# Attention with cached K and V, two problems on one core: first product in token halves, weights on a second DMA queue, half of x transposed by DMA

## The chip, the core and the metric

The kernel runs on one core of one Trainium2 chip. The metric is device time in microseconds (us), from launch to the last store. The engines: TensorE (in the profile PE for matmuls and PEld for weight loads, which overlap the matmuls), VectorE (DVE), ScalarE (ACT), GpSimd (POOL) and SyncE (SP). SP and ACT issue DMA transfers; SPq and ACTq are their queues in the profile, and PEq is TensorE's instruction sequencer. The granted clock is the share of TensorE's full clock that the profile records. A line number such as L306 is a line of the kernel; the changed kernel's lines stand four lower in the steady part (L306 becomes L302).

## The reference, cut to what matters

Two independent problems, A and B, each: 512 tokens (16 batches of 32) by 1024, 32 query heads, 4 K/V heads, 512 cached positions, head width 128, bf16.

```python
q = (x @ wq).reshape(B, Sq, Hq, Dh).transpose(0, 2, 1, 3)
scores = einsum("bhqd,bhkd->bhqk", q, repeat(k_cache)) * Dh ** -0.5
o = einsum("bhqk,bhkd->bhqd", softmax(scores), repeat(v_cache))
out = o.transpose(0, 2, 1, 3).reshape(B, Sq, Hq * Dh) @ wo
```

## The kernel before

The heads 0 to 7 of problem A are computed first ("the start"). After that a loop over 128 attention slots begins; each slot is scores, exponentials and values for one batch and one K/V head, and between them TensorE takes about seven matmuls per slot from one long stream: the query heads 8 to 31 of A, those of B, then the output products. Each query head has eight matmuls, one per chunk of 128 rows of wq. Weights arrive in blocks of four heads, 1 MB each.

The start loads x and the first weights on the sync queue. TensorE warms up on a tile of zeros, transposes all 32 blocks of x and multiplies as the chunks come in:

```python
load_x(0, slice(0, TT // 2)); load_x(0, slice(TT // 2, TT))
load_w0(slice(0, 1), slice(0, NF * DH // 2))          # NF = 6 heads early
...                                                   # the other chunks, x and w0 in turn
load_k(0, slice(0, 1))                                # K by DMA transpose
load_wq(0, 2)                                         # heads 8 to 11
load_k(0, slice(1, GRP)); load_v(0); load_k(1); load_v(1)

warm_up(19)
transpose_x(0, (2, 4))                                # 8 transposes on TensorE, copies on DVE and ACT
for dc in range(DC - 2):
    for h in range(NF):
        if dc % 2 and h == NF // 2:
            transpose_x(dc // 2 + 1)
        first_head(first_q[h], h, dc)
...                                                   # last two chunks, then heads 6 and 7 alone
```

The later loads follow a plan by slot. The stream of projections looks its weights up by name when it is built:

```python
def load_wq(pr, c4, ...):
    t = blk_tile([P, DC, 4 * DH], "wq_sb")
    ...                                               # one DMA of 1 MB
    wq_tiles[pr, c4] = t                              # replaces an older tile of that name

for c4 in range(3, 16):                               # block 3 holds heads 12 to 15
    need = (c4 - 2) * 4 * DC / 7.0
    at(max(0, int(need) - 10), load_wq, c4 // 8, c4 % 8)   # c4 = 3 comes at slot 0
```

## Time and profile before

| | before |
|---|---|
| median of 4 runs | 346.69 us (346.27 to 347.31) |
| profiled execution | span 344.8 us |
| TensorE busy | 336.7 us, 98% |
| head 8 begins (first matmul with wq_sb) | 20.44 us |
| TensorE stops for the block of heads 12 to 15 | 1.58 us, until 31.28 us |

From the page of the kernel before: the first line of the busy table, and the chain of work that ended last.

```profile
PE 336.7 (98%) x2098; PEld 214.2 (62%) x2137; DVE 267.3 (78%) x338; ACT 186.9 (54%) x210; POOL 46.7 (14%) x206
...
PE 89%; SPq 5%; DMA 3%; issue 1%; ACT 0%; ACTq 0%
PE f_ps L325 31%; PE q_ps L306 25%; PE ob L430 17%; PE s_ps L362 16%; SPq L280 4%; DMA wq_sb<-in_A_wq_dram 2%; DMA x_sb<-in_A_x_dram 1%; SPq L471 1%; SPq L468 0%; SPq L288 0%; SPq L250 0%; ACT o_sb L334 0%; SPq L697 0%; ACTq L334 0%
```

TensorE is the limit, but the 11% of the chain that are not TensorE are worth a look: queue issues (SPq, mostly the K transposes of L280) and two DMA landings. Nearly all of it lies in the start. The table of stretches of the kernel before, TensorE only (stretch, its length, busy time and instructions, granted clock, DMA share, GB/s), shows where TensorE is not full:

```profile
0.00:29.70 29.70, 28.26 (x170) 1.00 0.96 240
29.70:31.30 1.60, 0.02 (x1) 1.00 1.09 351
31.30:335.00 303.70, 301.81 (x1869) 1.00 0.87 210
```

After 31.3 us nothing is left to gain by a better start: TensorE is busy to the end. So the time is the moment at which it can go on with head 12, plus what follows (344.8 - 31.3 = 313.5 us). The timeline of the start of the kernel before (start, length, engine, line, operation; in brackets the idle time ahead and what ended it):

```profile
0.86 0.96 SPq L468 DMA_DIRECT2D x_sb<-in_A_x_dram  x2
1.08 2.21 PE L500 MATMUL warm_ps<-warm 128*128 128x128 bf16 x19 [1.08 <-DVE shift L237]
3.40 0.61 PE L514 MATMUL xT_ps<-ident,x_sb 128*128 128x128 bf16 x4
4.95 2.32 PE L526 MATMUL q_ps<-xT,w_sb 128*128 128x512 bf16 x9
...
20.44 1.24 PE L306 MATMUL q_ps<-xT,wq_sb 128*128 128x512 bf16 x5
24.48 3.80 SPq L250 DMA_DIRECT2D wq_sb<-in_A_wq_dram  x3
29.09 0.60 PE L362 MATMUL s_ps<-qT,kT 128*128 128x256 bf16 x4
31.28 1.69 PE L306 MATMUL q_ps<-xT,wq_sb 128*128 128x512 bf16 x7 [1.58 <-DMA wq_sb<-in_A_wq_dram]
```

x lands by 3.40 us, right as the 19 warm-up matmuls end. Head 8 begins at 20.44. The block for heads 12 to 15 is the first of the three issued from 24.48 on, and TensorE waits for it until 31.28.

### The profile page before, as it was taken

To read this page: it belongs to the slowest core of one execution; us is meant where nothing else is said; L and a number is where in the kernel's file an instruction comes from. 1 tells how busy PE (TensorE), PEld (TensorE's weight loads), DVE (VectorE), ACT (ScalarE), POOL (GpSimd) and SP (SyncE) were. 2 spreads that over 40 slices of the span, in tenths; PEclk is the share of its full clock that TensorE was granted. 3 is DMA by queue.
4 is the path that set the end of the run, shared out by engine and by line. 5 is a ranking of instruction groups with operands and counts; after the bars stand their busy time and mean duration, and the time that the engine had idled before them with its cause. 6 is when DMAs were issued, how large, how long until landed. Compare 5 with 4: busy or idle time off the path is not lost.

```text
span 344.8 us, 5491 instructions
## 1 busy us (share of the span) xinstructions
PE 336.7 (98%) x2098; PEld 214.2 (62%) x2137; DVE 267.3 (78%) x338; ACT 186.9 (54%) x210; POOL 46.7 (14%) x206
## 2 busy tenths in 40 slices
PE   8998999999999999999999999999999999999996
PEld 6554666666666666666666666666666666666555
DVE  1236888888988898888888898889888888888540
ACT  2346667667666666666654545554455555554010
POOL 0001110011111111111002212221222100111100
PEclk9999999999999999999999999999999999999999
DMA  6999989899997999999999956999649996440001
GB/s 193 307 174 347 231 241 274 172 290 261 300 273 162 227 243 225 215 214 307 268 282 254 238 137 175 345 248 228 117 107 290 334 187 170 106 109 0 17 18 33
DMA packets 126509, 71.70 MB, mean 208 GB/s; under 512 B 73744, under 2 KB 126224, under 8 KB 126480
## 3 DMA queue, kind: packets, MB, share of 16 engines
q1 hardware_dynamic: 125952, 70.20, 84.1%
q0 software_dynamic: 384, 1.05, 0.8%
q8 instruction: 17, 0.28, 0.4%
q14 instruction: 12, 0.10, 0.1%
q10 hardware_dynamic: 144, 0.07, 0.1%
HBM read 51.38 MB, written 2.10 MB: 155 GB/s over the span
## 4 chain that ended last, share of the span: by engine, by line
PE 89%; SPq 5%; DMA 3%; issue 1%; ACT 0%; ACTq 0%
PE f_ps L325 31%; PE q_ps L306 25%; PE ob L430 17%; PE s_ps L362 16%; SPq L280 4%; DMA wq_sb<-in_A_wq_dram 2%; DMA x_sb<-in_A_x_dram 1%; SPq L471 1%; SPq L468 0%; SPq L288 0%; SPq L250 0%; ACT o_sb L334 0%; SPq L697 0%; ACTq L334 0%
## 5 line engine op out<-in xcount | busy, mean ns | idle before, releaser
L370 ACT ACTIVATE p_sb<-s_ps,shift 128x1024 bf16<-128x1024 f32 x128 | 142.5, 1114 | 103.4 <-PE s_ps L362 85.5
L381 DVE TRANSPOSE_TENSOR_REDUCE parts<-p_sb 128x32 f32<-128x1024 bf16 x128 | 158.9, 1242 | 20.5 <-ACT p_sb L370 18.8
L325 PE MATMUL f_ps<-wo_sb,oT 128*128 128x512 bf16 (+1 forms) x525 | 127.5, 366 | 0.5
L306 PE MATMUL q_ps<-xT,wq_sb 128*128 128x512 bf16 x430 | 113.7, 379 | 2.2 <-DMA wq_sb<-in_A_wq_dram 1.6
L430 PE MATMUL ob<-p_sb,v_sb 128*128 128x256 bf16 x512 | 76.8, 273 | 0.8
L362 PE MATMUL s_ps<-qT,kT 128*128 128x256 bf16 x512 | 76.8, 273 | 0.0
L325 PEld LDWEIGHTS <-oT 128*128 128x128 bf16 x544 | 53.2, 98 | 36.0
L362 PEld LDWEIGHTS <-kT 128*128 128x128 bf16 x512 | 56.8, 113 | 28.6 <-DMA kT<-in_B_k_cache_dram 0.5
L306 PEld LDWEIGHTS <-wq_sb 128*128 128x128 bf16 x448 | 43.7, 98 | 33.4 <-DMA wq_sb<-in_A_wq_dram 1.8
L430 PEld LDWEIGHTS <-v_sb 128*128 128x128 bf16 x512 | 50.1, 98 | 20.0
L452 DVE TENSOR_TENSOR oT<-r,ob 128x512 bf16<-128x512 f32 x64 | 44.0, 687 | 23.4 <-PE ob L430 22.9
L416 DVE STREAM_TRANSPOSE r<-rall 128x512 f32<-128x512 f32 x64 | 44.2, 691 | 1.1
L314 ACT CAST qT<-q_ps 128x512 bf16<-128x512 f32 x56 | 32.6, 582 | 13.8 <-PE q_ps L306 13.8
L399 POOL COPY half<-cs 64x32 f32<-64x32 f32 x32 | 6.5, 204 | 230.6 <-DVE cs L389 230.6
L334 ACT CAST o_sb<-f_ps 128x512 bf16<-128x512 f32 (+1 forms) x17 | 9.5, 558 | 24.4 <-PE f_ps L325 16.7
L526 PE MATMUL q_ps<-xT,w_sb 128*128 128x512 bf16 x62 | 14.4, 383 | 0.2
L389 DVE TENSOR_REDUCE cs<-parts 128x32 f32<-128x128 f32 x32 | 12.1, 377 | 1.1
L411 DVE RECIPROCAL rall<-sums 128x32 f32<-128x32 f32 x32 | 10.2, 318 | 1.6 <-POOL sums L408 1.6
L520 DVE COPY xT<-xT_ps 128x512 bf16<-128x512 bf16 x4 | 1.7, 424 | 11.5 <-PE xT_ps L514 11.5
L526 PEld LDWEIGHTS <-w_sb 128*128 128x128 bf16 x64 | 6.2, 99 | 6.9 <-issue 0.5
L336 POOL DMA_DIRECT2D out_dram<-o_sb x8 | 4.6, 574 | 33.4 <-ACT o_sb L334 33.3
L400 POOL TENSOR_TENSOR half<-half,cs 64x32 f32<-64x32 f32 x32 | 7.8, 242 | 2.6
(26 smaller groups left out, 51.5 us busy)
## 6 DMA issues: line engine op xcount, KB each, us to landing
v_sb<-in_A_v_cache_dram SPq DMA_DIRECT2D x16, 512.0 KB, 4.4
wq_sb<-in_B_wq_dram SPq DMA_DIRECT2D x8, 1024.0 KB, 6.3
wo_sb<-in_A_wo_dram SPq DMA_DIRECT2D x8, 1024.0 KB, 7.5
v_sb<-in_B_v_cache_dram SPq DMA_DIRECT2D x16, 512.0 KB, 4.4
wo_sb<-in_B_wo_dram SPq DMA_DIRECT2D x8, 1024.0 KB, 8.2
wq_sb<-in_A_wq_dram SPq DMA_DIRECT2D x6, 1024.0 KB, 7.5
w_sb<-in_A_wq_dram SPq DMA_DIRECT2D x7, 192.0 KB, 4.9
kT<-in_A_k_cache_dram SPq DMA_TRANSPOSE x64, 4.5
```

The source lines that it names most:

```text
L280: nc.sync.dma_start_transpose(out=kT[:, q, :], in_=ks[q])
L306: nc.tensor.matmul(ps[:], lhsT=w[:, dc, (h % 4) * DH:(h % 4 + 1) * DH], rhs=xT[pr][:, dc, :], start=(dc == 0), stop=(dc == DC - 1),)
L314: nc.scalar.copy(out=qT[pr, g][:, :, hl, :], in_=ps[:].rearrange("p (b s) -> p b s", s=SQ),)
L325: nc.tensor.matmul(ps[:, 0:width], lhsT=oT[pr, tt][:, h, :], rhs=wo_tiles[pr, nh, h // REP][:, h % REP, off:off + width], start=(h == 0), ...
L362: nc.tensor.matmul(s_ps[:, c, :], lhsT=kT[:, i % GRP, c, :], rhs=qT[pr, g][:, b, :, :].rearrange("p h s -> p (h s)"), start=True, stop=True,)
L370: nc.scalar.activation(out=p_sb[:], in_=s_ps[:], func=ACTF.Exp, bias=shift[:], scale=SCALE)
L381: nc.vector.tensor_reduce(out=parts[k][:, q, :, :].rearrange("p c h -> p (c h)"), in_=st[i]["p"][:].rearrange("p c (h s) -> p (c h) s", s=SQ),
L389: nc.vector.tensor_reduce(out=cs[:], in_=parts.pop(k)[:].rearrange("p q c h -> p q h c"), axis=AX.X, op=ALU.add,)
L416: nc.vector.transpose(out=r[:].rearrange("p n s -> p (n s)"), in_=rall[:, k, o * 2 * REP:(o + 1) * 2 * REP] .unsqueeze(2).to_broadcast([P, ...
L430: nc.tensor.matmul(ob[j][:, q, :], lhsT=v_sb[:, i % GRP, c, :], rhs=st[i]["p"][:, c, :], start=(c == 0), stop=(c == KC - 1),)
L452: nc.vector.tensor_tensor(out=out, in0=rcp.pop(j)[:].rearrange("p (q h) s -> p q h s", h=REP), in1=ob.pop(j)[:].rearrange("p q (h s) -> p ...
L526: nc.tensor.matmul(q_ps, lhsT=w0[dc // HC][:, dc % HC, h * DH:(h + 1) * DH], rhs=xT[0][:, dc, :], start=(dc == 0), stop=(dc == DC - 1),)
```

## The change

Its intent is a shorter start: begin the product when half of the tokens of the first x chunk are there, take the first weights from ScalarE's queue so that they are issued beside x, transpose the last four chunks of x by DMA and not on TensorE, and let heads 6 and 7 join at the middle chunk. The block of heads 12 to 15 is also issued early. The core of the diff, cut:

```diff
-            warm = work.tile([P, P], BF16, name="warm", tag="p_sb", bufs=7)
-            nc.vector.memset(warm[:], 0.0)
+            warm = nc.const_aps.tensor(1.0, [P, P], BF16)
...
-            load_x(0, slice(0, TT // 2))
-            load_x(0, slice(TT // 2, TT))
-            load_w0(slice(0, 1), slice(0, NF * DH // 2))
...
+            load_w0(nc.scalar, 0, 1, 0, NF)
+            load_x(0, 0, TT // 2)
+            load_w0(nc.scalar, 1, 2, 0, NF)
+            load_x(0, TT // 2, TT)
+            load_x(2, 0, TT)
...
+            load_x_transposed(HC)
+            load_w0(nc.sync, HC + 2, DC, 0, REP)
+            load_x_transposed(HC + 2)
+            nc.scalar.preload_act_table_set("natural_log_exp_and_others")
             load_wq(0, 2)
+            load_k(0)
+            load_wq(0, 3)
+            load_k(1)
             load_v(0)
...
+            warm_up(23)
+            transpose_x(0, 0, TT // 2)
+            warm_up(3)
+            first_heads(range(0, NF // 2), (0,), 0, TT // 2)
+            transpose_x(0, TT // 2, TT)
+            first_heads(range(NF // 2, NF), (0,), 0, TT // 2)
+            first_heads(range(NF), (0,), TT // 2, TT)
...
+            first_heads(range(NF, REP), range(HC))
+            first_heads(range(REP), range(HC, DC - 2))
...
-                at(GRP * (j - 1) + 2, load_v, j)
+                at(GRP * (j - 1) + 2, load_v, j, 2 if j < 5 else 1)
             for c4 in range(3, 16):
                 need = (c4 - 2) * 4 * DC / 7.0
```

The last two lines are not changed: `load_wq(0, 3)` is new, and the plan's range still begins at 3.

## The prediction

> **What bounds the kernel now.** TensorE: the busy table gives it 336.7 of 344.8 us (98%), and the table by stretches 301.8 of the 303.7 us from 31.3 to 335 us, at granted clock 1.00. Only the start can be shortened. There the timeline shows first transposes 3.40, first product 4.95, head 8 (next weights) 20.2, first scores 21.5 us, and then one wait that matters: TensorE stops from 29.7 to 31.28 for the weight block (wq_sb) of heads 12 to 15, which the sync queue issued at 24.48. The chain of waits says the same: before 31.3 us it runs through sync queue issues (mostly kT transposes, 1.26 to 2.5 us each) and that 6.75 us load. The time is that landing plus a fixed 313 us.
>
> **What the change does.**
> 1. TensorE work at the start shrinks: 16 of 32 transposes go (eight cost about 0.45 us in the stream), -0.9 us; the product starts on the first token half, its weights on ScalarE's queue, about -0.5 us; small waits (0.4 and 0.2 us) may go. Estimate: head 8 at 18.3 to 19 us, unless the DMA-transposed chunks are late (needed near 11.8 and 15, estimated landing 11.5 to 13 and 14 to 15.5). TensorE would be ready for head 12 near 28 us.
> 2. The block for heads 12 to 15 is issued early, but the plan still loads it at slot 0, into a new tile that replaces the first. The instruction order shows that TensorE waits for the second copy and nothing reads the first. So 1 MB is loaded for nothing, ahead of k, v and the copy that counts: 3.1 us at the 340 GB/s that plain loads reached.
> 3. Half of x (0.5 MB) goes through DMA transposes: packets of 256 B took 18 ns against 27 ns for 512 B, so about 0.8 us more DMA time, and two more issues on the sync queue (estimate 2 us each, from 6.8 us for B's 1 MB x). Two early kT transposes each came with a stall of all DMA engines of about 1.2 us; there may be more. The Trainium skill, "DMA: Bandwidth & Descriptors", section "Issuing engines are not separate DMA queues", says a second issuing engine saves only issue time.
> 4. Split v loads and the constant for warm-up: nothing measurable.
>
> **On the critical path.** The landing of the second copy. Estimate: x and first weights through by 13 to 15 us (before 13.3), then 3 MB of wq, 1 MB of v, 1 MB of kT, about 17.6 us at the rates above, plus 0 to 3 us of stalls: 31.5 to 35 us against 31.25. TensorE's gain of 1.5 to 2 us becomes a longer wait there (3 to 5.5 us), and the whole is about 1 us slower. Later waits keep their slack.
>
> **Time.** 348.0 us, 8 in 10 between 345.3 and 351.0. Faster by over 2%: 0.01; within 2%: 0.96; slower by over 2%: 0.03.
>
> **What would show it.** Right: head 8 near 18.5; the wait for wq_sb grows to 3 us or more and ends after 31.3; HBM read 1 MB higher; then the same timeline, shifted. Wrong on 1: waits for xT or w0 of up to 1 us near 12 or 15 us. Wrong on 2: the second copy lands by 30 us and the kernel gains up to 2 us (345).
>
> **What would make it wrong.** The DMA engines had idle time while kT was issued (utilisation 0.2 to 0.5 near 24 to 26 us); if the wasted load only fills that, nothing lands later. Or the wait exceeds 3.4 us and the clock gate closes: the Trainium skill, "TensorE: Matmul & The Clock Gate", says an idle window of about 3.4 us halves the clock; no drop shows at 1.6 us. That adds 1 to 2 us.

## The result, and the profile after

| | before | after |
|---|---|---|
| median of 4 runs | 346.69 us | 347.37 us (346.76 to 347.82) |
| ratio | | 1.0017 (95%: 0.9993 to 1.0041) |
| first transposes of x | 3.40 us | 4.74 us |
| first product | 4.95 us | 5.52 us |
| head 8 begins | 20.44 us | 22.32 us |
| wait for heads 12 to 15, until | 1.58 us, 31.28 us | 1.24 us, 32.81 us |
| what follows, to the end of the span | 313.5 us | 313.2 us |

A ratio is the mean time of one kernel's runs over that of the other's runs of the same rounds, so it is not quite the ratio of the medians quoted. All runs in this document are within 1.5% of the fastest execution of the same kernel; I quote granted clocks where they differ within it.

From the page after, the same lines as before:

```profile
PE 339.6 (98%) x2128; PEld 215.1 (62%) x2128; DVE 266.7 (77%) x336; ACT 186.2 (54%) x209; POOL 47.1 (14%) x206
...
PE 97%; DMA 1%; ACT 1%; issue 0%; SPq 0%; ACTq 0%
PE f_ps L321 32%; PE q_ps L302 28%; PE ob L426 16%; PE s_ps L358 16%; PE q_ps L529 5%; DMA x_sb<-in_A_x_dram 1%; PE xT_ps L519 0%; ACT p_sb L366 0%; ACT qT L310 0%; ACT o_sb L330 0%; PE q_ps L511 0%; SPq L693 0%; ACTq L330 0%
```

The chain now looks free of the weight block. That is a trap. The two longest waits of the kernel after up to 40 us, of TensorE's matmuls, and then those of its weight loads over the whole span (engine, line, what it waited for, total us, times, longest):

```profile
PE q_ps L302 <- ACT p_sb L366: 1.2, 1, 1.2
PE xT_ps L519 <- DMA x_sb<-in_A_x_dram: 1.2, 1, 1.2
```

```profile
PEld L302 <- DMA wq_sb<-in_A_wq_dram: 1.5, 1, 1.5
PEld L519 <- DMA x_sb<-in_A_x_dram: 1.5, 1, 1.5
```

For one and the same stop the matmul's row names ScalarE and the weight load's row names the DMA. A matmul needs the weights that the load ahead of it puts in place, so the load's wait is the matmul's too. The exponential that is named ended at 32.77 us, just before the block landed, so the profile took it for the releaser; the instruction order has head 12 waiting on ScalarE only for the emptying of a bank of PSUM (the memory that TensorE writes to), long done by then. Which of the two is right is tested by run e1. The timeline of the start after:

```profile
0.82 0.91 ACTq L478 DMA_DIRECT2D w_sb<-in_A_wq_dram  x2
0.86 1.48 SPq L466 DMA_DIRECT2D x_sb<-in_A_x_dram  x3
0.93 2.62 PE L511 MATMUL q_ps<-const-bfloat16-1.0 128*128 128x128 bf16 x23 [0.93 <-PEq L682]
4.74 0.61 PE L519 MATMUL xT_ps<-ident,x_sb 128*128 128x128 bf16 x4 [1.19 <-DMA x_sb<-in_A_x_dram]
5.52 0.80 PE L529 MATMUL q_ps<-xT,w_sb 128*128 128x256 bf16 x3
6.54 3.40 PE L529 MATMUL q_ps<-xT,w_sb 128*128 128x256 bf16 x12
...
22.32 1.24 PE L302 MATMUL q_ps<-xT,wq_sb 128*128 128x512 bf16 x5
24.54 5.35 SPq L246 DMA_DIRECT2D wq_sb<-in_A_wq_dram  x3
30.97 0.60 PE L358 MATMUL s_ps<-qT,kT 128*128 128x256 bf16 x4
32.81 1.47 PE L302 MATMUL q_ps<-xT,wq_sb 128*128 128x512 bf16 x6 [1.24 <-ACT p_sb L366]
```

Two things went the other way than intended. First, x is issued at the same 0.86 us but TensorE gets it at 4.74, not 3.40; the warm-ups are over at 3.55 and there is a gap of 1.19 us. Second, the products that follow run at half speed. Single start times in the trace show 0.107 us per 128 columns and 0.427 us per 512 columns until 10.3 us after the span's start, and then 0.056 and 0.216. In the kernel before the change of pace comes at 5.5 us, and its record of the granted clock begins with 1.0 at 5.43. The Trainium skill, "TensorE: Matmul & The Clock Gate", Part 1, gives the two clocks as 1.2 and 2.4 GHz and says the faster one follows about 3.4 us of sustained activity. The factor of two agrees; the time only roughly, since from the first matmul to the change it took 4.35 us in the kernel before and 2.72 us in e11 below (1.08 to 3.80). Below, "the clock gate opens" means this change to full pace, and "closes" the way back. A trap here too: the mean granted clock of the run after is listed as 1.0, because its trace has no record of the clock at all.

In spite of this the total grew by only 0.7 us, because the slower start hides behind the wait: the block for head 12 landed only at 32.8.

### The profile page after: what moved, and what is told of

The parts are those of the page before. It is cut to its first block, busy times and chain, and to the rows that moved or that the text cites. A ratio compares the mean times of both kernels' runs of the same rounds, so it can differ in the third digit from the quotient of the medians.

```text
span 346.0 us, 5510 instructions
## 1 busy us (share of the span) xinstructions
PE 339.6 (98%) x2128; PEld 215.1 (62%) x2128; DVE 266.7 (77%) x336; ACT 186.2 (54%) x209; POOL 47.1 (14%) x206
## 3 DMA queue, kind: packets, MB, share of 16 engines
q0 software_dynamic: 384, 1.05, 0.8%
HBM read 51.90 MB, written 2.10 MB: 156 GB/s over the span
## 4 chain that ended last, share of the span: by engine, by line
PE 97%; DMA 1%; ACT 1%; issue 0%; SPq 0%; ACTq 0%
PE f_ps L321 32%; PE q_ps L302 28%; PE ob L426 16%; PE s_ps L358 16%; PE q_ps L529 5%; DMA x_sb<-in_A_x_dram 1%; PE xT_ps L519 0%; ACT p_sb L366 0%; ACT qT L310 0%; ACT o_sb L330 0%; PE q_ps L511 0%; SPq L693 0%; ACTq L330 0%
## 5 line engine op out<-in xcount | busy, mean ns | idle before, releaser
L321 PE MATMUL f_ps<-wo_sb,oT 128*128 128x512 bf16 (+1 forms) x544 | 131.8, 366 | 0.0
L302 PE MATMUL q_ps<-xT,wq_sb 128*128 128x512 bf16 x448 | 117.6, 379 | 1.2 <-ACT p_sb L366 1.2
L529 PE MATMUL q_ps<-xT,w_sb 128*128 128x512 bf16 (+1 forms) x70 | 16.2, 396 | 0.0
L529 PEld LDWEIGHTS <-w_sb 128*128 128x128 bf16 x70 | 7.4, 108 | 7.2 <-issue 0.3
L554 DVE CAST qT<-q_ps 128x512 bf16<-128x512 f32 x4 | 2.8, 692 | 9.6 <-PE q_ps L529 9.5
```

The costliest lines, as they stand in the source:

```text
L302: nc.tensor.matmul(ps[:], lhsT=w[:, dc, (h % 4) * DH:(h % 4 + 1) * DH], rhs=xT[pr][:, dc, :], start=(dc == 0), stop=(dc == DC - 1),)
L321: nc.tensor.matmul(ps[:, 0:width], lhsT=oT[pr, tt][:, h, :], rhs=wo_tiles[pr, nh, h // REP][:, h % REP, off:off + width], start=(h == 0), ...
L529: nc.tensor.matmul(first_q[h][:, ts], lhsT=w0[dc // HC][:, dc % HC, h * DH:(h + 1) * DH], rhs=xT[0][:, dc, ts], start=(dc == 0 and t0 == 0 ...
```

## The experiments

Three batches, each on one chip; "before" is the kernel before on that chip. All results were correct. The columns: first transposes of x, when the clock opens (from the trace's clock record, or from the pace of the matmuls where marked p), head 8, the wait for heads 12 to 15 and its end, from one profiled execution; then the median, and the ratio to before.

| run | x | clock | head 8 | wait, until | median us | ratio (95%) |
|---|---|---|---|---|---|---|
| e1_one_copy | 4.82 | 10.0 | 22.23 | none | 346.22 | 0.9976 (0.9956 to 0.9995) |
| e2_more_warm | 4.91 | 4.1 | 20.21 | 2.98, 32.44 | 349.03 | 1.0068 (1.0027 to 1.0110) |
| e3_both | 4.82 | 3.8 | 20.11 | none | 344.36 | 0.9939 (0.9917 to 0.9961) |
| e4_before_two_copies | 3.31 | 5.7 | 20.50 | 2.94, 32.69 | 350.05 | 1.0090 (1.0066 to 1.0113) |
| e5_before_early_copy | 3.27 | 5.6 | 20.39 | none | 344.94 | 0.9910 (0.9873 to 0.9947) |
| e6_x_first | 4.68 | 10.0 | 22.15 | none | 346.08 | 0.9938 (0.9900 to 0.9975) |
| e7_x_then_half | 3.72 | 4.2 | 19.85 | none | 346.15 | 0.9935 (0.9893 to 0.9978) |
| e8_fill_wait | 4.65 | 4.2 | 19.92 | 1.35 after the filler, 32.87 | 347.71 | 0.9988 (0.9950 to 1.0025) |
| e9_one_queue | 3.56 | 3.8 p | 19.93 | none | 344.38 | 0.9929 (0.9915 to 0.9942) |
| e10_both_again | 4.84 | 5.2 | 20.24 | none | 344.38 | 0.9928 (0.9915 to 0.9942) |
| e11_before_early_again | 3.10 | 3.8 | 20.35 | none | 345.19 | 0.9952 (0.9938 to 0.9967) |

Before was 346.79 us in the first batch (e1 to e4), 347.51 in the second (e5 to e8) and 347.00 in the third (e9 to e11).

One kernel's clock does not open at the same moment in every execution: e3 and e10 are the same kernel (3.8 and 5.2 us), and so are e5 and e11 (5.6 and 3.8). But the three traces with a gap of over 1.1 us ahead of the first transposes (after, e1, e6) are the three that open at 10 us or later; the ten others open by 5.7.

### e1_one_copy: the wasted load taken out

```diff
-            for c4 in range(3, 16):
+            for c4 in range(4, 16):
```

> The changed kernel without the plan's second load of the block for heads 12 to 15. Theory L (the landing of the second copy sets the time): TensorE's wait of 1.2 us for wq_sb near 32 us vanishes, TensorE is ready for head 12 near 31.6 and goes on, so the time is 1.2 us under the changed kernel, about 0.5 us under the kernel before (346.2). Theory C (the cold start of TensorE sets the time, the copy only fills idle DMA): no change from the changed kernel, 347.3.

Measured: 346.22 us, 1.15 us under the changed kernel's 347.37, though in another batch of runs (four of its six executions took 346.0 to 346.8 us, two 345.2). The waits of TensorE's matmuls in e1 up to 40 us are only these two:

```profile
PE xT_ps L519 <- DMA x_sb<-in_A_x_dram: 1.3, 1, 1.3
PE q_ps L511 <- PEq L682: 0.9, 1, 0.9
```

The stop near 32 us is gone, with the exponential still in its place. So the releaser was the second copy of the block, and the row that named ScalarE was wrong. Theory L holds, as far as the changed kernel's 1.2 us go.

### e2_more_warm: the gap bridged, both copies kept

```diff
-            warm_up(23)
+            warm_up(37)
```

> The changed kernel with 37 warm-up matmuls for 23, to bridge the gap from 3.3 to 4.7 us in which TensorE waits for x; second copy kept. Both theories: the products reach 0.216 us each by 8 us at the latest instead of 10.3, head 8 starts about 2 us earlier (near 20). Theory L: the block still lands near 32.8, the wait grows from 1.2 to about 3 us, time unchanged within 0.4 us. Theory C: about 2 us faster than the changed kernel, 345.3.

Measured: 349.03 us. Head 8 begins at 20.21, 2.1 us earlier, so the warm-up did what it should, and nothing was gained: the block landed at 32.44 and the wait grew to 2.98 us. That is theory L. From its timeline:

```profile
20.21 1.24 PE L302 MATMUL q_ps<-xT,wq_sb 128*128 128x512 bf16 x5
32.44 1.68 PE L302 MATMUL q_ps<-xT,wq_sb 128*128 128x512 bf16 x7 [2.98 <-DMA wq_sb<-in_A_wq_dram]
```

Not expected was that it became slower. The six executions with their granted clocks: 347.44 and 347.48 at 0.999; 349.10 at 0.994; 349.31 at 0.995; 352.52 at 0.988; and the profiled one, 348.95 at 1.0, which has a second wait of 1.3 us, for K of problem B at 191 us. Without a lowered clock and that wait, it is the changed kernel's time.

### e3_both: one copy and the gap bridged

Both edits above. 

> Both edits. Theory L: now the start of TensorE counts, 3 to 3.5 us faster than the changed kernel, about 344.2. Theory C: same as more warm-up alone, 345.3. If neither edit does anything: 347.4.

Measured: 344.36 us, as theory L has it. The timeline of e3 beside the one shown of after:

```profile
4.82 0.40 PE L519 MATMUL xT_ps<-ident,x_sb 128*128 128x128 bf16 x4 [0.28 <-DMA x_sb<-in_A_x_dram]
6.06 1.90 PE L529 MATMUL q_ps<-xT,w_sb 128*128 128x256 bf16 x12
20.11 1.24 PE L302 MATMUL q_ps<-xT,wq_sb 128*128 128x512 bf16 x5
```

The same twelve matmuls take 1.90 us instead of 3.40. The cold start was worth 1.9 us (346.22 to 344.36), but only once the wait was out of the way: of the two corrections the first alone gained 1.15 us, the second alone nothing, both together 3.0. Five of e3's six executions lie between 344.1 and 344.5 us; the sixth took 346.28, like e1, and has no trace.

### e4_before_two_copies: the kernel before with the wasted load alone

```diff
             load_k(0, slice(1, GRP))
+            load_wq(0, 3)
             load_v(0)
```

> The kernel before with nothing but the wasted load: the block for heads 12 to 15 also loaded after the first kT, never read. Theory L with DMA as the limit: the copy that counts lands up to 3.1 us later than 31.28 and the kernel is 1.5 to 3 us slower than before (348.2 to 349.7). Rival (the load fills idle time of the DMA engines while the sync queue issues kT): under 0.7 us slower.

Measured: 350.05 us, 3.3 us over before. The copy that counts landed at 32.69 instead of 31.28, 1.4 us later, which is less than half of the 3.1 us that 1 MB takes at 340 GB/s. The table of stretches over all engines, from 18 to 26 us, first of before and then of e4 (the last two figures are DMA share and GB/s):

```profile
18.00:26.00 8.00, 8.00 (x44) 4.30 (x43) 2.69 (x3) 3.76 (x5) 0.00 (x0) 1.00 0.77 172
```

```profile
18.00:26.00 8.00, 8.00 (x45) 4.32 (x44) 2.63 (x3) 3.77 (x5) 0.00 (x0) 1.00 1.00 277
```

While the sync queue issued K, the DMA engines of the kernel before had room: 105 GB/s more over 8 us is 0.84 MB. The wasted load filled idle time first, and delayed the rest by 1.4 us. So both my theory and its rival were half right on the landing, and the time is above what either expected. I had overlooked where these 1.4 us arise. The sync queue came to the copy that counts at 25.87 us instead of 24.48, and from there it took 6.8 us in both kernels:

```profile
25.87 3.77 SPq L250 DMA_DIRECT2D wq_sb<-in_A_wq_dram  x3
```

In the changed kernel it is the other way: the copy was issued at 24.54, almost as in the kernel before, and took 8.3 us to land. So e4 matches its delay (1.5 us) in size, and not the way in which it comes about.

The other 1.9 us come mostly from the clock. The stretches of e4, TensorE only (the figure after the instruction count is the granted clock):

```profile
28.00:32.00 4.00, 1.75 (x11) 1.00 1.06 357
32.00:36.00 4.00, 3.31 (x10) 0.63 1.09 348
36.00:40.00 4.00, 4.00 (x26) 0.95 1.24 286
```

After the wait of 2.94 us the clock went to half for 3.41 us (33.02 to 36.43 in its record), which costs 1.7 us. Five of six executions of e4 have a clock of 0.993 to 0.995, which is what 3.41 us at half speed make of the mean (1 - 0.5 x 3.41 / 348 = 0.995); they took 349.6 to 351.2 us, and the one at 1.0 took 348.40.

The length of a wait alone does not decide this: the 2.94 us of e4 closed the gate, the 2.98 us of e2's profiled execution did not. In every trace with a clock record, a stretch of full clock that ends inside the record is a whole number of 3.413 us long (8 and 91 of them in e4, 98 in e1, 99 in e3, 101 in e2). So the clock seems to be set once per such window. In e4 the wait lay within one window, 29.61 to 33.02 us; in e2 a boundary at 31.40 us (4.09 + 8 x 3.413) cut it into 1.93 and 1.04 us. That this decides is an inference from two traces and was not tested.

### e8_fill_wait: matmuls put into the wait

e2 and this:

```diff
+                if (pr, h) == (0, 12):
+                    for _ in range(40):
+                        nc.tensor.matmul(ps[:, 0:P], lhsT=warm, rhs=warm, start=True, stop=True)
                 for dc in range(DC):
```

> The changed kernel with 37 warm-ups and both copies (349.0 us in its run, with a granted clock of 0.988 to 0.995 in half of its executions), plus 40 idle matmuls (about 2.2 us) ahead of head 12, inside the wait for the second copy. If the long wait closes the clock gate and that is what made more warm-up slower than the changed kernel: clock 0.998 or more in all executions and about 347.4. If the slow executions come from later landings: still near 349 with the same spread.

Measured: 347.71 us, executions from 347.32 to 348.13, clocks of 0.999 and 1.0 in all six. The block landed at 32.87, no earlier than in e2; only the idle time was filled. So the long wait closing the clock gate is what made e2 slower than the changed kernel, as far as six executions can tell: a lowered clock in none here, in three of six in e2.

### e6_x_first: a run that did not do what it was meant to

```diff
+            nc.scalar.preload_act_table_set("natural_log_exp_and_others")
             load_w0(nc.scalar, 0, 1, 0, NF)
...
-            nc.scalar.preload_act_table_set("natural_log_exp_and_others")
```

with one copy of the block, as in e1. 

> The changed kernel with one copy of the block, 23 warm-ups, and ScalarE's activation-table load put ahead of its two weight loads, so that these issue 1.3 us later. Theory S (the weight loads on ScalarE's queue share the DMA engines with the first half of x and delay it): x lands near 3.4 us instead of 4.8, the gap in TensorE's work shrinks from 1.2 to under 0.3 us, products warm by 8 us at the latest, and the time is 2 to 3 us under the same kernel with the old order (346.2), near 343.7. Rival (x is late for another reason, its tile or its smaller rows): x still lands near 4.8, time 346.2.

Measured: 346.08 us, as e1. It looks like a verdict for the rival, and is none, as two lines of its timeline show:

```profile
0.82 1.28 ACT L483 ACT_TABLE_LOAD   x1 [0.82 <-PEq L682]
0.85 0.91 ACTq L478 DMA_DIRECT2D w_sb<-in_A_wq_dram  x2
```

The table load ran on the engine while ScalarE's queue issued the DMAs at 0.85 us all the same. The order in the program moved nothing. The run is a repeat of e1, and says nothing on why x is late.

### e7_x_then_half: the first 96 KB of weights behind x

```diff
-            load_w0(nc.scalar, 0, 1, 0, NF)
             load_x(0, 0, TT // 2)
-            load_w0(nc.scalar, 1, 2, 0, NF)
+            load_w0(nc.sync, 0, 1, 0, NF // 2)
             load_x(0, TT // 2, TT)
+            load_w0(nc.scalar, 0, 1, NF // 2, NF)
+            load_w0(nc.scalar, 1, 2, 0, NF)
```

with one copy and the table load first. 

> As the run with x first, and the weights that the first product needs (three heads of chunk 0, 96 KB) issued by the sync queue right behind the first half of x. Theory S: first product by 4.3 us instead of 5.5, 343.0 to 343.7; no better than x first alone if the first product was not waiting for weights there.

Measured: x at 3.72 us, with ScalarE's first load still issued at 0.85, but in rows of 768 bytes instead of 1536. The first product came at 5.13, not by the expected 4.3, held up 0.62 us by its weights, and the median of 346.15 us is no better than e6. The executions fall in two groups, 343.96 and 344.06, and four from 345.93 to 346.74. The profiled one is of the first group and opened its clock at 4.2 us. That the others opened theirs a window later is likely, since they stand 2.3 us off, but no trace of one was taken.

### e9_one_queue: ScalarE's queue left empty

```diff
-            load_w0(nc.scalar, 0, 1, 0, NF)
             load_x(0, 0, TT // 2)
-            load_w0(nc.scalar, 1, 2, 0, NF)
+            load_w0(nc.sync, 0, 1, 0, NF // 2)
             load_x(0, TT // 2, TT)
+            load_w0(nc.sync, 0, 1, NF // 2, NF)
+            load_w0(nc.sync, 1, 2, 0, NF)
```

with one copy and warm-ups 25 and 5. 

> The changed kernel with one copy of the block, nothing loaded on ScalarE's queue: the sync queue issues the first half of x, the weights of three heads of chunk 0, the second half of x, the other three heads, chunk 1; warm-ups 25 and 5 for 23 and 3. Theory S (the weight loads on ScalarE's queue delay x): x lands near 3.4 us, first product near 4.3, no gap over 0.3 us in TensorE's work before it, products warm by 8 us at the latest, head 8 between 18.6 and 19.8: 343.0 to 344.0. Rival (x is late for another reason): x near 4.7 and, with a gap of over 1 us, about 346.2 in most executions.

Measured: 344.38 us, above the 343.0 to 344.0 expected. From its timeline:

```profile
0.93 2.84 PE L512 MATMUL q_ps<-const-bfloat16-1.0 128*128 128x128 bf16 x25 [0.93 <-PEq L683]
3.56 0.50 PE L520 MATMUL xT_ps<-ident,x_sb 128*128 128x128 bf16 x4
4.33 0.49 PE L530 MATMUL q_ps<-xT,w_sb 128*128 128x256 bf16 x3
13.03 7.07 PE L530 MATMUL q_ps<-xT,w_sb 128*128 128x512 bf16 x32 [0.31 <-DMA xT<-in_A_x_dram]
19.93 1.24 PE L302 MATMUL q_ps<-xT,wq_sb 128*128 128x512 bf16 x5
```

There is no wait ahead of the first transposes. The two halves of x took 2.2 us from issue to landing (median), against 4.1 in the changed kernel; the lines of the two DMA views, first of after and then of e9:

```profile
x_sb<-in_A_x_dram SPq DMA_DIRECT2D x2, 128.0 KB, 4.1
```

```profile
x_sb<-in_A_x_dram SPq DMA_DIRECT2D x2, 128.0 KB, 2.2
```

So the early weights on ScalarE's queue are what delayed x. The run empties that queue and puts the first half of x ahead of all weights at once; whether the same weights ahead of x on the sync queue would have delayed it as much was not tested. But the 1.2 us that this won on the first product were lost again: with one queue the later weights and the transposed x come later (the queue issues its two x transposes at 5.84 and 8.58 us instead of 4.80 and 7.46), and TensorE waits for them and for K. Head 8 began at 19.93, just outside what I expected.

### e5, e10 and e11: what the new start is worth

e5 and e11 are the kernel before with the block loaded once and early:

```diff
             load_k(0, slice(1, GRP))
+            load_wq(0, 3)
             load_v(0)
...
-            for c4 in range(3, 16):
+            for c4 in range(4, 16):
```

> The kernel before with the block for heads 12 to 15 issued once, after the first kT, and not at slot 0. If that landing sets the time of the kernel before too, the wait of 1.6 us vanishes: 345.2, against 346.8 before. What is then left between this and the changed kernel with both edits (344.4) is what the new start itself is worth: about 0.8 us.

> The kernel before with the block loaded once and early, again: 344.9. If the new start with its queue split is worth 0.3 us or more, this is the slower of the two repeats; if head 8 at 20.1 instead of 20.4 is lost in the spread, they are equal.

e10 is e3 once more. 

> The run with both edits (one copy, 37 warm-ups) again, on the chip of its neighbours: 344.4 as before.

Measured: 344.94 us for e5, and on the third chip 345.19 for e11 against 344.38 for e10. So the largest part of what e3 gains over before, about 2 us, needs two lines in the kernel before and nothing of the new start. The new start with its gap bridged is worth about 0.7 us more (means of 345.03 and 344.35 us; the intervals of the two ratios overlap slightly). Their traces show little of it: head 8 begins at 20.24 us in e10 and 20.35 in e11, and the spans are 342.6 and 342.8 us. The traced execution of e11 is its fastest, so where the rest of the 0.7 us arises is not known. e3 and e9 are the best versions, 0.6 to 0.7% faster than before and also faster than the changed kernel.

In the second batch 5 of the 11 executions of the kernel before itself had a clock of 0.994 or 0.995 and took 348.7 to 349.6 us, against one of 12 and none of 9 in the other two. It flatters the ratios of that batch. That it is the same closing of the gate, in its own wait for the block, fits the numbers; no trace of such an execution was taken. No execution of e5 or e11, which have no such wait, is below 0.998.

Not tested by themselves are the transposing of half of x by DMA, the new order of the K and V loads and the split V loads.

## Why the prediction was right or wrong

- **The time** (348.0, range 345.3 to 351.0; measured 347.37) and its reason were right: the landing of the second, useful copy of the block sets the time. It was put at 31.5 to 35 us and came at 32.81, and 313 us followed. e1 shows that it held TensorE, e2 that a faster start behind it gains nothing. That the number came so close is partly luck: TensorE was ready for head 12 at 31.57 us, not near 28, and 1.24 us more would have made the start and not the landing set the time.
- **"So 1 MB is loaded for nothing [...] 3.1 us"** was too much. e4 shows 1.4 us for the wasted load alone, and the landing in the changed kernel is 1.5 us later than before. The prediction named the reason under what could make it wrong: idle time while K was issued.
- **"Head 8 at 18.3 to 19 us"** was wrong: it was 22.32. The step that failed is "the product starts on the first token half, its weights on ScalarE's queue, about -0.5 us". With the weights on the second queue TensorE got x 1.3 us later than in the kernel before (4.74 against 3.40; in e9, without them, at 3.56 with no wait), which opened a gap between warm-up and work; TensorE then ran at half clock until 10.3 us. That the gap caused the late opening is shown by e3 (clock at 3.8 us with the gap bridged, 4.82 us for x as in e1). I had cited that a second issuing engine saves only issue time, and had not asked what the shared engines do to the order of landing.
- **"The wait becomes a longer wait there (3 to 5.5 us)"** was wrong for the same reason: with TensorE itself ready only at 31.57 us (30.97 + 0.60), 1.24 us of it were left. In e2 it was 2.98.
- **16 transposes less, -0.9 us:** not contradicted, and not shown by itself. From first transposes to head 8 it takes 15.3 us in e3 (20.11 - 4.82) and 15.4 in e10; in the kernel before 17.0 (20.44 - 3.40), and 17.25 in e11, whose clock opened as early as e3's. So the path from x to head 8 is 1.7 us or more shorter, for all its changes together. But x comes 1.4 to 1.7 us later, and of the difference 0.1 to 0.3 us are left at head 8.
- **x chunks by DMA transpose late, a wait of up to 1 us:** not seen in the changed kernel, whose TensorE was late itself. It appears, with 0.31 us, in e9.
- **HBM read 1 MB higher:** 51.38 to 51.90 MB, so 0.52 MB. The counter leaves out what is read by DMA transposes: all inputs are 69.2 MB, and less all of K and B's x (17.8 MB) that is 51.4. The wasted block adds 1.05 MB and half of A's x, now transposed by DMA, takes 0.52 away.
- **The clock gate closing on a longer wait** was named as a risk of 1 to 2 us. The changed kernel's wait was 1.24 us, and its runs show no sign of it. In e4 the trace shows it, with 3.41 us at half clock, so 1.7 us; in e2 the mean clock of three of six executions does (0.994, 0.995 and 0.988).

## What to carry to other kernels

When a load is moved earlier, look whether a plan still issues it: a tile that nothing reads costs bandwidth ahead of the loads that count, and the profile shows only a later landing. A second DMA queue did not start the product earlier here (5.52 us, against 4.95): the large transfers on it slowed the small one that everything waits for (4.1 us to land, against 2.2). Put first what is needed first, and let warm-up work last until it has landed. Two faults in a row hide each other: correcting the one that is covered gains nothing (and here even cost something, as a longer wait can close the clock gate), so correct both before judging either.

## What the Trainium skill lacked or had wrong

- "TensorE: Matmul & The Clock Gate", "HAM oscillation": it advises against idle gaps of more than about 3.4 us (the table at the end of the page says about 3). Here a wait of 2.94 us was enough in e4, where the clock went to half 0.33 us after the wait had ended, and one of 2.98 us was not in e2, so the length alone is no safe rule. What agrees is the length of the slow stretch, 3.41 us.
- "DMA: Bandwidth & Descriptors", "Issuing engines are not separate DMA queues": it says that transfers issued from several engines interleave and that a second engine saves issue time. It does not say what this does to the other queue's first transfer: 128 KB of x took 4.1 us to land beside two loads of 192 KB on ScalarE's queue, and 2.2 us without them. "Queues, rings and completion order" on the same page has the DMA engines alternate between queues packet by packet; the profile's packets of x, of 512 bytes, beside those of the weights, of 1536, could fit that (the page's packet is a bundle of descriptors and need not be the profile's), and in e7, with 768 and half the bytes, x came at 3.72 us instead of 4.74. That the packet size is the reason was not tested by itself.
- No page that I found: the profile's HBM read counter leaves out DMA transposes, as the sums above have it (51.38 MB of 69.2 MB of inputs).
- No page that I found: a trace without a record of the granted clock is listed with a mean of 1.0, though the matmuls ran at half pace until 10.3 us (0.427 us for 512 columns, then 0.216).
